# A two-layer mixture of experts behind a packed attention: the first half played from a list of 300 steps

## The chip, the cores and the metric

The kernel runs on one core of a Trainium2 chip. Its time is the device time of one execution in microseconds (us); lower is better. All arithmetic is in 32-bit floats. TensorE takes fp32 operands for transposes, scores and small products, and its own rounded form (fp32r) for the expert layers, where every operand is split into a high and a low part and three products are summed.

## What is computed

```python
# q, k, v: (4, 8, 576, 64), p: (4, 8, 32, 64)
p_packed = sm_attn(p, k, v)              # 32 packed queries over 576 keys
x = sm_attn(q, p_packed, p_packed)       # 576 queries over 32 packed keys
x = x.transpose(0, 2, 1, 3).reshape(2304, 512)

logits = x @ w_gate                      # layer 1: 8 experts, top 1, capacity 576
expert = argmax(logits); gate = softmax(logits)[expert]
# in order of rows, a row is kept while its expert has taken fewer than `capacity`
x = gate * (relu(x @ w1[expert]) @ w2[expert])     # 0 for rows that are dropped

logits = x @ w_gate2                     # layer 2: 8 experts, top 1, no capacity
expert = argmax(logits); gate = softmax(logits)[expert]
eom = sigmoid(x @ w_output_gate)[expert]
out = gate * eom * (relu(x @ w1b[expert]) @ w2b[expert])
```

## The kernel before

The four batches go through the attention one after another. `load` brings k, q (three pieces each) and v of a batch, `transp` transposes a piece on TensorE and copies it out of PSUM. `s1_mm`, `s1_max`, `s1_exp` and `s1_rs` are the first softmax; `a1_T` transposes its result, `pp_mm` multiplies it with v, `pp_scale` divides by the sums and `pp_T` transposes the packed rows to `ppT`. The second softmax goes in two halves of 4 heads: `s2_mm`, `s2_tr` (a transpose in 32x32 blocks), `s2_max`, `s2_sub`, `s2_exp`, `s2_sum`, `s2_mul`, `s2_back`; its result is `a2T`. `g1_g`, `g1_l` and `g1_t` make the logits of the first gate; `ga`, `ga2`, `gb`, `gc`, `gd` choose the expert of each row, its rank and whether it is kept, and the expert that a batch needs.

The main path takes it that the kept rows of a batch all go to one expert and that only batch 0 and one more batch have any; with these inputs that is so, and the rest stands behind the test at the end. The expert part is done for two slots: batch 0 (its expert is `e0`) and the batch that `route` finds (`slots_i`). In layer 1 of the experts `moe1_ppw` multiplies `ppT` with a quarter of w1 (four quarters), and `layer1` multiplies that with `a2T` into one of eight tiles of `h`. `moe1_layer2` makes one of four tiles of `y` out of `h` and w2, which `split` cuts into `w2ah` (ScalarE) and `w2al` (GpSimd or VectorE). The second expert layer follows for batch 0, then for the other slot; `moe2_layer2` writes 128 rows of the output, the last block of a slot with `osb` copied by ScalarE and stored by a transfer of the SyncE queue.

Every engine runs its instructions in the order in which they are written, and so does the SyncE queue, which starts all transfers. The order is written by hand: `att_iter`, `att_last` and `att_end` hold the steps of neighbouring batches, interlocked; `FL()` puts one piece of expert layer 1 between steps of the last attention. All PSUM tiles come from one ring of four (`psm`), all raw weights from one ring of four buffers (`raw_p`). At the end an `If` on `flag_i` would run the remaining slots and a general path; its condition does not hold here, and every engine jumps over the body.

Of the kernel before, what the change touches and what calls it, by code (L numbers as in the profile page):

```python
# [8 lines left out]
FP32 = mybir.dt.float32  # L9
# [14 lines left out]
def tr(nc, out, in_, ident):  # L24
    return nc.tensor.transpose(out, in_, ident)  # L25


@with_exitstack
def tile_kernel(
# [124 lines left out]
    sp = [ENG.SP]  # L154
# [202 lines left out]
    def pp_scale(b):  # L357
        pps = ab_p.tile([128, 2, 2, D], FP32, tag="pps", name="pps")
        pp, sm = at.pop(("pp", b)), at.pop(("sm", b))
        for G in range(2):  # L360
            nc.vector.tensor_scalar(
                pps[:, G], pp[:, G, 0:D].unsqueeze(1).to_broadcast([128, 2, D]), sm[:, G:G + 1], None,
                op0=ALU.mult)
        at["pps", b] = pps

    def pp_T(b):
# [4 lines left out]
        nc.vector.tensor_copy(ppT[:, b], ps[:, :, 0:128])  # L371
# [22 lines left out]
    def s2_sub(b, G, eng):  # L394
        eng.tensor_tensor(sv(b, G), sv(b, G), bc(at.pop(("mx", b, G)), 32), op=ALU.subtract)
# [11 lines left out]
    def s2_mul(b, G, eng):  # L407
# [90 lines left out]

    def split(src, nm, i, lo_eng):

        wp = mp["ws2"] if i == 3 else mp["ws"]
        hi = wp.tile([128, 1024], FP32R, tag="w", name=nm + "h")
        lo = wp.tile([128, 1024], FP32R, tag="w", name=nm + "l")
        s = src.rearrange("p a b -> p (a b)")
        nc.scalar.activation(out=hi, in_=s, func=ACTF.Copy)  # L505
        lo_eng.tensor_tensor(lo, s, hi.bitcast(FP32), op=ALU.subtract)  # L506
        a = src.shape[1]
        return tuple(t.rearrange("p (a b) -> p a b", a=a) for t in (hi, lo))
# [9 lines left out]
    def moe1_load1(e):  # L518

        ws = []  # L520
        for fq in range(F // 256):
# [6 lines left out]
    def moe1_load2(e):  # L528
        ws = []
        for dh in range(2):  # L530
            for kh in range(2):
                w = raw(4, 256)
                nc.sync.dma_start(
                    w, w2a[bass.ds(e, 1), kh * 512:(kh + 1) * 512, dh * 256:(dh + 1) * 256].rearrange(
                        "o (k p) d -> p (o k) d", p=128))
                ws.append(w)
        return ws

    def moe1_x(a2, lo_eng):
# [23 lines left out]
    def chain(ps, seq, mid={}):  # L563
# [673 lines left out]
```

## Time and profile before

| what | value |
|---|---|
| median of 3 runs | 276.68 us (275.87 to 277.39) |
| profiled execution | 277.06 us, of which 275.0 us from the first to the last instruction (span) |
| TensorE (PE) | 249.9 us busy, 91% of the span |
| VectorE (DVE) | 130.6 us, 47% |
| ScalarE (ACT) | 100.6 us, 37% |
| GpSimd (POOL) | 44.5 us, 16% |
| granted TensorE clock | 0.97 of full on the mean |

A busy share is a mean over stages: attention to 59 us, experts' first layer to 161 us, second layer to the end. The page's slices show where they differ: TensorE is 90% or more busy in nearly every slice from 135 us on, and the transfers keep the DMA engines busy above 90% only up to 41 us. What a change in the first half is worth is read from the waits and the clock of that half.

### The profile page before, as it was taken

The numbers are of one execution on the slowest core, as the hardware profiler recorded it, in microseconds if no ns is written. First come the engines' busy times: TensorE is split into PE (matmuls) and PEld (weight loads), VectorE is DVE, ScalarE is ACT, GpSimd is POOL, SyncE is SP. The second block draws the span as 40 slices with busy tenths as digits, with TensorE's granted clock in tenths as the row PEclk, the third lists the DMA queues.
The fourth block names the chain that finished last, engine by engine and source line by source line (L and its number), as shares of the span: only waits on it lengthen the run. The fifth ranks groups of instructions, "written<-read, shape, count | busy, mean of one in ns | idle before, by whom it ended". The sixth has DMA issues, their size and how long they took to land. (4 is left out here: it accounts for less than half of the span.)

```text
span 275.0 us, 6065 instructions
## 1 busy us (share of the span) xinstructions
PE 249.9 (91%) x2529; PEld 218.4 (79%) x2529; DVE 130.6 (47%) x316; ACT 100.6 (37%) x152; POOL 44.5 (16%) x69
## 2 busy tenths in 40 slices
PE   7789889929989989997999999999999999999970
PEld 5567657707886979786999999999888999988850
DVE  0234776985995684369712333487031435610000
ACT  3586847623470310445502232263140414410020
POOL 5001514532350330006420000000020000002000
PEclk9999999986999999999799999999999999999995
DMA  6999990067320005943696224008201360001211
GB/s 195 395 331 382 396 390 31 6 215 247 87 69 2 0 0 184 301 135 118 156 257 221 79 76 153 2 14 252 80 23 73 119 229 2 0 0 39 61 42 45
DMA packets 29652, 37.17 MB, mean 135 GB/s; under 512 B 4144, under 2 KB 21168, under 8 KB 29616
## 3 DMA queue, kind: packets, MB, share of 16 engines
q1 hardware_dynamic: 29616, 36.69, 40.6%
q8 instruction: 22, 0.36, 0.6%
q14 instruction: 14, 0.11, 0.1%
HBM read 31.25 MB, written 4.72 MB: 131 GB/s over the span
## 5 line engine op out<-in xcount | busy, mean ns | idle before, releaser
L21 PE MATMUL o<-w2bh,h 128*128 128x512 f32 x144 | 45.9, 391 | 0.0
L21 PE MATMUL y<-h,w2ah 128*128 128x288 f32 x256 | 44.6, 296 | 0.0
L21 PEld LDWEIGHTS y<-h,w2ah 128*128 128x128 f32 x256 | 37.6, 189 | 0.0
L584 DVE SCALAR_TENSOR_TENSOR h<-h 128x576 fp32r<-128x576 f32 (+3 forms) x64 | 25.8, 447 | 24.7 <-ACT h L577 24.7
L577 ACT ACTIVATE h<-h 128x576 fp32r<-128x576 f32 x32 | 20.4, 651 | 36.3 <-PE h L21 32.5
L21 PEld LDWEIGHTS o<-w2bh,h 128*128 128x128 f32 x144 | 26.9, 188 | 5.7
L21 PE MATMUL o<-w2bl,h 128*128 128x512 f32 x80 | 31.3, 391 | 0.0
L21 PE MATMUL y<-h,w2al 128*128 128x288 f32 x128 | 27.7, 297 | 0.8 <-DVE w2al L506 0.8
L21 PE MATMUL h<-yh,w1bh 128*128 128x288 f32 x128 | 27.5, 296 | 0.0
L21 PE MATMUL h<-yh,w1bl 128*128 128x288 f32 x128 | 27.4, 295 | 0.0
L21 PE MATMUL h<-yl,w1bh 128*128 128x288 f32 x128 | 27.3, 295 | 0.0
L241 ACT ACTIVATE T<-tp 128x768 f32<-128x768 f32 x24 | 19.9, 850 | 11.4 <-PE tp L25 11.4
L21 PEld LDWEIGHTS y<-h,w2al 128*128 128x128 f32 x128 | 20.5, 188 | 1.5 <-DVE w2al L506 1.0
L25 PE MATMUL tp<-ident,r 128*128 128x128 f32 x144 | 20.1, 283 | 1.6 <-DMA r<-in_k_dram 1.2
L506 POOL TENSOR_TENSOR w2al<-wraw,w2ah 128x1024 fp32r<-128x1024 f32 x6 | 14.2, 2389 | 44.1 <-ACT w2ah L505 44.1
L683 POOL TENSOR_SCALAR osb<-osb,g 64x512 f32<-64x512 f32 x2 | 3.1, 1570 | 111.0 <-DVE osb L682 61.4
L21 PEld LDWEIGHTS h<-yh,w1bh 128*128 128x128 f32 x128 | 20.6, 189 | 0.2
L21 PEld LDWEIGHTS h<-yh,w1bl 128*128 128x128 f32 x128 | 20.6, 188 | 0.0
L21 PEld LDWEIGHTS h<-yl,w1bh 128*128 128x128 f32 x128 | 20.6, 188 | 0.0
L25 PEld LDWEIGHTS tp<-ident,r 128*128 128x128 f32 x144 | 16.3, 144 | 5.1 <-issue 1.2
L593 ACT ACTIVATE yh<-y 128x576 fp32r<-128x576 f32 x8 | 5.2, 651 | 40.8 <-PE y L21 40.8
L594 DVE TENSOR_TENSOR yl<-y,yh 128x576 fp32r<-128x576 f32 x8 | 6.0, 755 | 27.3 <-ACT yh L593 27.3
(173 smaller groups left out, 378.0 us busy)
## 6 DMA issues: line engine op xcount, KB each, us to landing
wraw<-in_moe_w_dram SPq DMA_DIRECT2D x32, 512.0 KB, 4.8
r<-in_k_dram SPq DMA_DIRECT2D x12, 384.0 KB, 7.2
r<-in_q_dram SPq DMA_DIRECT2D x12, 384.0 KB, 8.7
v<-in_v_dram SPq DMA_DIRECT2D x4, 1152.0 KB, 8.4
out_dram<-zt SPq DMA_DIRECT2D x2, 1152.0 KB, 7.5
out_dram<-osb SPq DMA_DIRECT2D x8, 256.0 KB, 2.0
a2s<-a2T SPq DMA_DIRECT2D x1, 576.0 KB, 5.4
p_sb<-in_p_dram SPq DMA_DIRECT2D x4, 64.0 KB, 6.9
```

What stands on the lines that cost most here:

```text
L21: return nc.tensor.matmul(out, lhsT=lhsT, rhs=rhs, start=start, stop=stop)
L25: return nc.tensor.transpose(out, in_, ident)
L241: nc.scalar.activation(out=o, in_=i, func=ACTF.Copy)
L506: lo_eng.tensor_tensor(lo, s, hi.bitcast(FP32), op=ALU.subtract)
L577: nc.scalar.activation(out=hi, in_=ps[:, :, 0:HS], func=ACTF.Relu)
L584: nc.vector.scalar_tensor_tensor(o, i, 0.0, a.bitcast(FP32), op0=ALU.max, op1=ALU.subtract)
L593: nc.scalar.activation(out=half(y[0][:, c, :]), in_=ps[:, :, 0:HS], func=ACTF.Copy)
L594: nc.vector.tensor_tensor(half(y[1][:, c, :]), ps[:, :, 0:HS], half(y[0][:, c, :]).bitcast(FP32), op=ALU.subtract)
L683: nc.gpsimd.tensor_scalar(o[:n], o[:n], g2[:n, t:t + 1], None, op0=ALU.mult)
```

## The change

The body from the first load to the end of the second slot's expert layer 1 is no longer a sequence of calls in functions but a list, `PLAN`, of 300 names. `STEPS` maps a name to a call (`tk00`: transpose piece 0 of k of batch 0; `y014`: slot 0, y tile 1, products of row block 4), and a loop plays the list. The steps are the same pieces of work, some cut finer: a load is one piece, `split` is `high` and `low` apart, `moe1_layer2` is eight steps for the eight blocks of `h` and one that copies out. A letter at a step's end names an engine (A: ScalarE, D: VectorE, none: the default, GpSimd for `s2_sub`, `s2_mul` and the low halves, VectorE for `pp_scale` and `pp_T`, ScalarE for `a1_T`).

```diff
+PLAN = """
+warm4 warm9 warm7 k00 tk00 k01 tk01 k02 tk02 p0 dup0 pT0 k10 tk10 p1 dup1 sa00 ma00 ea00 sa01 ma01 k12 ea01 rs0 pT1
+k11 tk11 tk12 at00D q00 tq00 v0 q01 at01D pp00 pp01 sc0A q02 k21 tq01 k20 tq02 pt0A sa10 q10 ma10 ea10 sa11 p2 ma11
...
-    def pp_scale(b):
+    def pp_scale(b, eng=1):
         pps = ab_p.tile([128, 2, 2, D], FP32, tag="pps", name="pps")
         pp, sm = at.pop(("pp", b)), at.pop(("sm", b))
         for G in range(2):
...
+            if eng == 0:
+                nc.scalar.activation(out=pps[:, G], in_=i, func=ACTF.Copy, scale=sm[:, G:G + 1])
+            else:
+                nc.vector.tensor_scalar(pps[:, G], i, sm[:, G:G + 1], None, op0=ALU.mult)
...
-        nc.vector.tensor_copy(ppT[:, b], ps[:, :, 0:128])
+        evac(eng, ppT[:, b], ps[:, :, 0:128])
...
+    def y_mm(ps, h, w, c, kk):
...
+        for x, (i, j) in enumerate(((0, 0), (0, 1), (1, 0))):
+            for u in range(2):
+                mm(nc, ps[:, u, 0:HS], w[i][:, kk % 4, ds_], h[j][:, kk, HSL[u]],
+                   kk == 0 and x == 0, kk == NF - 1 and x == 2)
...
-            nc.scalar.activation(out=o[:n], in_=ps[:n, 0, :], func=ACTF.Copy, scale=g2[:n, t:t + 1])
+            w = DM // 2 if last else DM
+            nc.scalar.activation(out=o[:n, 0:w], in_=ps[:n, 0, 0:w], func=ACTF.Copy, scale=g2[:n, t:t + 1])
+            if last:
+                nc.vector.tensor_scalar(o[:n, w:], ps[:n, 0, w:], g2[:n, t:t + 1], None, op0=ALU.mult)
...
-        nc.sync.dma_start(
+        (nc.scalar if last else nc.sync).dma_start(
...
-        warm(16)
...
-        def att_iter(b):
...
+        for t in PLAN.split():
...
+            STEPS[n](*a)
...
+        bs1_act = val(slots_i[0:1, 0, 0:1], B - 1, ENG.Activation)
         for t in order:
-            moe2_layer2(h, ws, t, g2_1, bs1)
+            last = t == order[-1]
+            moe2_layer2(h, ws, t, g2_1, bs1_act if last else bs1, last)
...
-    with tc.If(rest > 0, preferred_fallthrough_block=False):
+    with tc.If(rest > 0):
```

The list also names engines. `pp_scale` and `pp_T` of batches 0, 2 and 3 go from VectorE to ScalarE. `a1_T` was on ScalarE in its first part and on VectorE in its second for batches 0 to 2; now it is on VectorE for batch 0 and for the first part of batch 1, and on ScalarE otherwise. One low half of w2 of slot 0 instead of two is on VectorE, and the low half of `x` of the second slot goes from VectorE to GpSimd. The 20 warm-up matmuls are all at the start. K of batch 3 is loaded ahead of v of batch 2. The y tiles of slot 0 come in the order 1, 2, 0, 3, woven into one another, and the logits of batches 1 to 3 are ahead of them and not inside.

**VectorE before**, from the index of batch 0's expert (`e_i`) to the packed rows of batch 3 (`pps`, `ppT`), in the last attention:

```order
L220 CAST e_i<-pe_136 1x1
L329 TENSOR_SCALAR sm<-sm 128x2
L330 RECIPROCAL sm<-sm 128x2
L411 STREAM_TRANSPOSE a2T<-sT 128x2x288
L383 STREAM_TRANSPOSE sT<-s 128x576
L402 TENSOR_REDUCE dn_1097<-sT 128x18
L403 TENSOR_SCALAR dn_1097<-dn_1097 128x18
L404 RECIPROCAL dn_1097<-dn_1097 128x18
L391 TENSOR_REDUCE mx_1149<-sT 128x18
L361 TENSOR_SCALAR pps<-pp,sm 128x128 x2
L371 COPY ppT<-ppTp 128x256
```

**ScalarE in the changed kernel**, the same place: batch 2's `pps` to the first copies of expert layer 1 (`wh`, `h`):

```order
L379 ACTIVATE pps<-pp,sm 128x128 x2
L257 ACTIVATE T<-tp 128x3x128x2
L257 ACTIVATE a1T<-a1Tp 128x640
L257 ACTIVATE a1T<-a1Tp 128x512
L257 ACTIVATE ppT<-ppTp 128x256
L257 ACTIVATE T<-tp 128x3x128x2 x3
L379 ACTIVATE pps<-pp,sm 128x128 x2
L416 ACTIVATE sT<-sT 128x576
L257 ACTIVATE ppT<-ppTp 128x256
L591 ACTIVATE wh<-ppw 128x512 x2
```

The packed rows of batches 2 and 3 have left VectorE's row behind the softmax work and stand on ScalarE, ahead of the experts' first copies.

**VectorE before**, second slot's layer 1, the choice of batch 0's second expert (`c`, `eq`, `pe`, `e_0`) among the copies of `h`:

```order
L584 SCALAR_TENSOR_TENSOR h<-h 128x576
L195 TENSOR_REDUCE c_1965<-cp 1x8
L203 TENSOR_REDUCE m<-c_1965 1x1
L205 TENSOR_TENSOR eq<-c_1965,m 1x8
L206 SCALAR_TENSOR_TENSOR eq<-eq,revv 1x8
L207 TENSOR_REDUCE pe_1969<-eq 1x1
L208 TENSOR_SCALAR pe_1969<-pe_1969 1x1
L220 CAST e_0_1978<-pe_1969 1x1
L214 TENSOR_REDUCE tot<-c_1965 1x1
L215 TENSOR_TENSOR mu_138<-tot,m 1x1
L584 SCALAR_TENSOR_TENSOR h<-h 128x576
L560 TENSOR_TENSOR wl<-ppw,wh 128x512
```

**VectorE in the changed kernel**, the same choice:

```order
L614 SCALAR_TENSOR_TENSOR h<-h 128x576 x3
L211 TENSOR_REDUCE c_2096<-cp 1x8
L219 TENSOR_REDUCE m<-c_2096 1x1
L221 TENSOR_TENSOR eq<-c_2096,m 1x8
L222 SCALAR_TENSOR_TENSOR eq<-eq,revv 1x8
L223 TENSOR_REDUCE pe_2100<-eq 1x1
L224 TENSOR_SCALAR pe_2100<-pe_2100 1x1
L236 CAST e_0_2109<-pe_2100 1x1
L230 TENSOR_REDUCE tot<-c_2096 1x1
L231 TENSOR_TENSOR mu_138<-tot,m 1x1
L626 TENSOR_TENSOR yl<-y,yh 128x576 x2
```

It stood between copies of `h`; now all eight copies of `h` are ahead of it.

**ScalarE before**, the end of the program, from the second slot's block of 64 rows on:

```order
L681 ACTIVATE osb<-o 64x512
L675 ACTIVATE osb<-o,g_1_2558 128x512 x3
L1194 TENSOR_LOAD flag_i
L1195 COMPARE_AND_BRANCH
L1195 UNCONDITIONAL_BRANCH
```

**ScalarE in the changed kernel**, the same end:

```order
L723 ACTIVATE osb<-o 64x512
L715 ACTIVATE osb<-o,g_1_2559 128x512 x2
L715 ACTIVATE osb<-o,g_1_2559 128x256
L726 ISA
L726 DMA out_dram<-osb 128x512
L1061 TENSOR_LOAD flag_i
L1062 COMPARE_AND_BRANCH
```

The last block is copied in half by ScalarE, which also starts its transfer, and the unconditional branch behind the test is gone from here: it stands behind the body, at the program's end. On the other engines the branch moves in the same way.

## Rows read from the trace of the kernel before

**Rows 1.** Five stretches: length, then busy us (instructions) by engine, granted clock, DMA.

```profile
core 0: us, PE busy (x) PEld busy (x) DVE busy (x) ACT busy (x) POOL busy (x), PEclk, DMA share, GB/s
4.30:40.20 35.90, 30.90 (x633) 22.58 (x631) 16.19 (x38) 22.74 (x38) 6.77 (x14) 1.00 1.03 376
40.20:59.00 18.80, 14.29 (x436) 11.49 (x433) 15.93 (x43) 10.38 (x16) 7.40 (x7) 1.00 0.17 60
59.00:80.40 21.40, 19.66 (x209) 16.25 (x210) 17.11 (x33) 11.29 (x18) 9.11 (x9) 0.84 0.55 175
80.40:135.80 55.40, 51.04 (x421) 45.22 (x419) 37.17 (x99) 18.18 (x31) 11.34 (x6) 0.97 0.36 111
135.80:266.70 130.90, 130.86 (x825) 120.70 (x823) 44.02 (x105) 36.04 (x50) 6.46 (x4) 1.00 0.29 90
```

**Rows 2.** Waits of TensorE, 0 to 140 us: total us, times, longest.

```profile
PE ppTp L25 <- DVE pps L361: 3.7, 1, 3.7
PE s L21 <- ACT T L241: 3.2, 3, 1.4
PE h L21 <- DVE h L584: 2.4, 1, 2.4
PE cp L21 <- DVE K L478: 1.2, 1, 1.2
```

**Rows 3.** Timeline of VectorE, 51 to 131 us: start, us, instruction.

```profile
51.96 2.62 DVE L206 SCALAR_TENSOR_TENSOR eq<-eq,revv 1x8 f32<-1x8 f32 x1
...
54.97 0.14 DVE L220 CAST e_i<-pe 1x1 int32<-1x1 f32 x1
...
124.86 2.34 DVE L205 TENSOR_TENSOR eq<-c,m 1x8 f32<-1x8 f32 x1
127.24 2.31 DVE L206 SCALAR_TENSOR_TENSOR eq<-eq,revv 1x8 f32<-1x8 f32 x1
...
130.26 0.74 DVE L584 SCALAR_TENSOR_TENSOR h<-h 128x576 fp32r<-128x576 f32 x1
```

**Rows 4.** Timeline of GpSimd, 41 to 136 us.

```profile
51.87 2.69 POOL L543 TENSOR_TENSOR xl<-a2T,xh 128x1152 fp32r<-128x1152 f32 x1
...
124.79 4.74 POOL L506 TENSOR_TENSOR w2al<-wraw,w2ah 128x1024 fp32r<-128x1024 f32 x2 [26.31 <-ACT w2ah L505]
```

**Rows 5.** Groups by form, ScalarE 4.3 to 60 us: count, busy us, mean ns.

```profile
L241 ACT ACTIVATE T<-tp 128x768 f32<-128x768 f32 x23 | 19.0, 849 | 11.4 <-PE tp L25 11.4
```

**Rows 6.** Groups by form, VectorE 40 to 86 us.

```profile
L361 DVE TENSOR_SCALAR pps<-pp,sm 128x128 f32<-128x128 f32 x4 | 1.2, 340 | 0.0
L371 DVE COPY ppT<-ppTp 128x256 f32<-128x256 f32 x2 | 0.8, 425 | 1.2 <-PE ppTp L25 1.2
```

**Rows 7.** Timelines: SyncE's first expert-weight transfer, TensorE's first expert product.

```profile
56.12 0.98 SPq L523 DMA_DIRECT2D wraw<-in_moe_w_dram  x2
...
59.90 0.45 PE L21 MATMUL ppw<-wraw,ppT 64*32 64x256 f32 x8 [0.30 <-DMA wraw<-in_moe_w_dram]
```

**Rows 8.** Timeline, end of the program.

```profile
266.26 0.40 PE L21 MATMUL o<-w2bl,h 128*128 128x512 f32 x1
266.75 0.69 ACT L675 ACTIVATE osb<-o,g 128x512 f32<-128x512 f32 x1 [4.52 <-PEq L1195]
267.46 0.33 SPq L684 DMA_DIRECT2D out_dram<-osb  x1
```

**Rows 9.** Sequencers, branch (L1195) and end (L1232): ns min/median/max, first and last start.

```profile
L1195 SPq EVENT_SEMAPHORE  x9: 17/17/17, 268.0 to 270.9; - x9
...
L1195 ACTq COMPARE_BRANCH  x2: 38/41/44, 267.3 to 267.6; - x2
...
L1195 SPq COMPARE_BRANCH  x2: 38/48/57, 267.8 to 271.0; - x2
...
L1232 SPq EVENT_SEMAPHORE  x10: 17/28/28, 273.7 to 275.0; - x10
...
L1232 ACTq DRAIN  x2: 8/44/81, 270.8 to 274.5; - x2
```

More of the change, by code (lines that the diff above doesn't have):

```diff
@@ L153, in tile_kernel @@
     HSL = [slice(0, HS), slice(HS, S)]
-    sp = [ENG.SP]
     def bc(ap, n):
@@ L516, in new_h, with moe1_load1 @@
         return h[:, :, 0:S], h[:, :, S + (LAST if last_first else 0):], h
-    def moe1_load1(e):
+    def moe1_load1(e, pieces=range(4)):
         ws = []
-        for fq in range(F // 256):
+        for fq in pieces:
             w = raw(4, 256)
@@ L595, in moe1_layer2 @@
             half(y[1][:, c, :]), ps[:, :, 0:HS], half(y[0][:, c, :]).bitcast(FP32), op=ALU.subtract)
+    def moe1_layer2(h, ws, c, y):
+        ps = psm("y")
+        for kk in range(NF):
+            y_mm(ps, h, ws[2 * (c // 2) + kk // 4], c, kk)
+        y_out(ps, c, y)
     def new_y(slot):
@@ L662, in moe2_load2, with moe2_layer2 @@
         return ws
-    def moe2_layer2(h, ws, t, g2, bsel):
+    def moe2_layer2(h, ws, t, g2, bsel, last=False):
         n = 128 if t < NT - 1 else LAST
@@ L1091, in tile_kernel @@
-        y0 = new_y(0)
-        def logits():
-            g1_l(1, B)
-        def onehots():
-            g1_t(1, B)
-            ga2(1, ga(1, B, "a1"))
-        def ranks():
-            gb(1, B)
-            gc(1, B, "a1")
-        def slots():
-            st["rest1"] = gd(1, B, "a1")
-            st["slots"] = route()
-        moe1_layer2(st["h"], ws, 0, y0, {14: logits, 18: onehots})
-        att_r.close()
-        pr = pool_in(moe, side="right", reuse_waits="tile")
-        mp["ws2"] = pr("ws2", 4)
@@ L1141, in tile_kernel, with gate_index, gate_rest, close_left @@
-        for i in (2, 3):
-            bz = val(slots_i[0:1, 0, i - 1:i], B - 1)
+        st, pw, wp, x1, h1, y = {}, {}, {}, {}, {}, {}
+        def gate_index():
+            st["e0"] = val(to_int(pe1[:, 0:1], "e0_i")[0:1, 0:1], E - 1)
+        def gate_rest(b0, b1):
+            st["r", b0] = gd(b0, b1, f"a{b0}")
+        def close_left():
+            att.close()
+            pm = pool_in(moe, reuse_waits="tile")
+            mp["y"] = pm("y", 1)
+            mp["ws"] = pm("ws", 10)
+        def close_right():
+            att_r.close()
+            pr = pool_in(moe, side="right", reuse_waits="tile")
+            mp["ws2"] = pr("ws2", 4)
+            mp["o"] = pr("o", 2)
@@ new lines, in tile_kernel @@
+        for t in PLAN.split():
+            n = t.rstrip("DAP") if t[-1] in "DAP" and t[-2].isdigit() else t
+            a = [int(x) for x in n.lstrip("abcdefghijklmnopqrstuvwxyzPT")]
+            n = n.rstrip("0123456789")
+            if t[-1] in "DAP" and t[-2].isdigit():
+                a.append({"A": 0, "D": 1}[t[-1]] if n in ("at", "sc", "pt") else V[t[-1]])
+            STEPS[n](*a)
+        slots_i, nb_f = st["slots"]
+        bs1, gs_1, y0, h, e2_0, g2_0 = st["bs"], st["gs"], y[0], h1[1], st["e2"], st["g2_0"]
@@ L1147, in tile_kernel @@
+        ws = [wp[1, i] for i in range(4)]
         e20 = val(e2_0[0:1, 0:1], E - 1)
```

354 lines of the change are left out of this document (92 added, 262 removed).

## Prediction

> **What bounds the kernel now.** I read the table of stretches first [rows 1]. From 135.8 us to the last matmul TensorE is busy 130.86 of 130.90 us at full clock; the change touches no step there but the last output block, so that half stays as long as it is. Everything before 135.8 us is open: TensorE is busy 30.90 of 35.90 us, then 14.29 of 18.80, 19.66 of 21.40 (at a granted clock of 0.84) and 51.04 of 55.40 (at 0.97). The first of these stretches is one in which the DMA engines are full (share 1.03). In the second they stand nearly idle (0.17), and still TensorE waits: the experts' weights can be asked for only when the index `e_i` of batch 0's expert is known, at 54.97 us [rows 3]. SyncE starts the first of them at 56.12 us and the first expert product runs at 59.90 us, behind that transfer [rows 7]. TensorE's waits up to 140 us, read next [rows 2], name three more places: 3.7 us once on VectorE's `pps`, 3.2 us in three waits on ScalarE's `T`, 2.4 us once on VectorE's `h`. The bound is therefore TensorE's amount of work, plus gaps in the first half where in-order queues of VectorE and ScalarE hold it up, plus slower clock around these gaps, plus 8.3 us between the last matmul's end (266.26 + 0.40 [rows 8]) and the span's end at 275.0 us.
>
> The sum goes against the profiled execution: 277.06 us, of which the span is 275.0; the median of the runs is 276.68, so 0.4 us is taken off at the end.
>
> **Term a, the start of the expert layer (59.9 us now).** Before 59.0 us TensorE has 30.90 + 14.29 us of work behind its start at 4.3, so it can't be done before 49.5 us; that is the lower end, 10.4 us earlier than 59.9. What held it is (1) `e_i`, found by a VectorE row that also carries the softmax work and batch 2's `pps` and `ppT`, and (2) the 3.7 us wait on `pps`. The list moves both: `pps` and `ppT` of batches 2 and 3 go to ScalarE, which removes the wait on VectorE's row, and the chain to `e_i` comes ahead of batch 3's last steps. From `e_i` to the first product now takes 59.90 - 54.97 = 4.9 us; with `e_i` at an estimated 43 us (right behind the last transfers of the first stretch, which are at their end at about 41) the weights are there by about 48, ahead of TensorE. Before, the operation L206 on that chain took 2.62 us while GpSimd's `xl` ran from 51.87 to 54.56 [rows 3, 4]; in the list `xl` of batch 0 stands behind `ei`, so that this hold leaves the chain.
>
> What is late next is ScalarE. It did 22.74 + 10.38 = 33.1 us before 59.0 [rows 1], of which 19.0 are 23 copies `T` at 849 ns [rows 5]. It gains six `pps` (priced by VectorE's 340 ns each: 2.0 us) and three `ppT` (425 ns: 1.3 us) [rows 6] and the second parts of `a1_T`, less the two that it gives up. That is 37 to 40 us of work which begins at about 6 us: done by 43 to 46 if it never waited, and it waits on each of TensorE's groups. The upper end is that only the 3.7 us wait goes and 0.8 of it comes back in ScalarE's own row: the start at 57, 2.9 us earlier. I take 52.0, nearer to the TensorE floor than to 57, since TensorE's own waits in these rows (3.7 and 3.2) and the late index account for most of the gap and each is addressed: **-7.9 us** (ends -10.4 and -2.9).
>
> **Term b, 59.0 to 80.4 us.** At a clock of 0.84 over 21.4 us, 0.16 x 21.4 = 3.4 us of full-speed work is lost, right behind the gaps of the stretch before; and one wait on `T` is 1.4 us [rows 1, 2]. Without the gaps both go, 4.8 us at most. Against that stands VectorE: it did 15.93 + 17.11 = 33.0 us between 40.2 and 80.4 [rows 1]. Of this 2 x (2 x 0.34 + 0.425) = 2.2 moves to ScalarE and 2.5 of L206's hold goes, but now about 27 us of it must be finished before the logits of batches 1 to 3, which the list puts ahead of the `y` tiles instead of inside one. That ends at 67 to 74 us, where TensorE with 15.7 us of expert work behind 52.0 arrives at 67.7. I charge 3 us for this backlog: **-1.8 us** (ends -4.8 and +1.0). The 24 products of the logits move, they aren't saved.
>
> **Term c, 80.4 to 135.8 us.** TensorE waits 2.4 us for `h` and 1.2 us for the operand `K` [rows 2]; at a clock of 0.97, 0.03 x 55.4 = 1.7 us is lost. The wait on `h` has a plain cause in the rows: VectorE's L205 and L206, the choice of batch 0's second expert, took 2.34 and 2.31 us for 8 numbers each, beside GpSimd's two `w2al` from 124.79 us of 4.74 us each, and the next copy of `h` could run only at 130.26 [rows 3, 4]. All eight copies of `h` stand ahead of that choice now. What is queued behind it is the low half of the second slot's last `y` tile and, on SyncE, the loads of the next weights, which are wanted some 25 us later: free. Sum removed: 5.3. New is a wait on ScalarE: `xh` of the second slot needs a copied `a2T` of a batch that is known only after `slots_i`; behind it in ScalarE's row stands the copy of the third `y` tile, which frees a PSUM buffer. From the weights' row, an index to its data is 4.9 us; I charge 1.5: **-3.8 us** (ends -5.3 and +1.0).
>
> The list also puts `xl` of the second slot and one more `w2al` on GpSimd, beside which VectorE's small operations were seen at 2.3 to 2.6 us instead of the 0.14 of a small CAST next to them [rows 3, 4]. [...]
>
> **Term d, the end.** The last matmul ends at 266.66; ScalarE copies it in 0.69, SyncE starts the store at 267.46 [rows 8], its waits L1195 follow to 270.9 with the last COMPARE_BRANCH at 271.0, and the next thing on SyncE is at 273.7, 2.7 us later, on the far side of the jump [rows 9]. The span ends at 275.0. So three pieces stand in line: store 3.5, jump 2.7, end 1.3. With the branch turned back the body is the fallthrough and every engine takes the jump at the test. ScalarE starts the store itself, reads the flag and jumps while the transfer is under way; SyncE, with no store of its own, reached the test long before. ScalarE's instructions after the test ran from 267.6 to the DRAIN at 270.8, 3.2 us; the copy by halves saves at most 0.25. ScalarE is thus at the end some 5.3 us behind the last matmul, the landing comes at about 4, and with the closing 0.5 to 1 the end is at 5.6 to 6.0 us instead of 8.3: **-2.4 us** (ends -2.8 and 0, when a second fetch at the end block takes the place of the removed one).
>
> [...]
>
> **Sum.** -7.9 - 1.8 - 3.8 - 2.4 = -15.9; 277.06 - 15.9 = 261.2, and 0.4 less for the median: **260.8 us**. With all lower ends (-23.3) it is 253.4, with all upper ends (-0.9) 275.8; half-way combinations give 257 to 265.5, the forecast's own range.
>
> **The rivals.**
> - *TensorE never waits.* ScalarE keeps ahead and VectorE's backlog is done in time: terms at -9.9, -4.0, -5.0 and -2.4 make -21.3, so 255.4 us (253.5 to 257). For it: over 4.3 to 59.0 us VectorE is busy 32.1 and ScalarE 33.1 of 54.7 us [rows 1], and the DMA share of 0.17 says that data is not the limit from 42 us. Against it: DMA is full up to 41 us, and in the second stretch VectorE is busy 15.93 of 18.80. Chance 0.22.
> - *The waits change places.* ScalarE's row with `pps`, `ppT` and `a1T` now stands between TensorE's groups as VectorE's did, and the late softmax halves hold the logits: term a is -5.0, b and c give nothing, d holds. -7.4, so 269.3 us (265.5 to 271). Against it: ScalarE has 21.6 of these 54.7 us free. Chance 0.20.
> - *The new end doesn't do what it says* (two jumps, two fetches): 263.2, within the forecast's range; a chance of 0.25 inside it.
> - *Slower: gaps that cost clock.* The pieces of batch 2 and 3, the expert's pieces and the logits are woven in one row; each gap that a late VectorE piece leaves in TensorE's row between 50 and 120 us costs its wait and the slower stretch behind it. Two such pairs are in the rows: 2.4 us with 1.7 of lost clock, and 3.7 with 3.4 [rows 1, 2], 4.1 to 7.1 together, 5.6 on the mean. It decides from three of them on (15.9 / 5.6 = 2.8); with four the time is 260.8 + 22.4 = 283 us. For it: VectorE's 33 us of backlog and the moved logits. Against it: the two gaps of before came from one cause each, which the list removes. Chance 0.04.
>
> **How the numbers follow.** Forecast with its own range 257 to 265.5: 0.50; TensorE never waits 0.22; waits change places 0.20; slower 0.04; between the last two, a change within 0.5% (1.4 us, about what a measurement of this kernel can tell from no change): 0.04. The first three are faster, 0.92 together. The range reaches from the first rival's 253.5 to most of the second's: 253.5 to 270.5.
>
> **What would show it.** The first expert product starts at about 52 us (a), with no wait on `pps`; a granted clock of 0.97 or more from there (b); no wait over 1.5 us on `h` (c), so that the dense second half begins at about 121 to 123 us; the last matmul's end to the span's end is about 6 us (d). [...] Any clock below 0.9 between 55 and 120 us would say that gaps are left which I didn't see.

## The result and the profile after

The changed kernel took 268.41 us (median of 4 runs, 266.27 to 269.92) against 276.44 us of the kernel before (275.87 to 277.39): a ratio of 0.970 with a 95% interval of 0.961 to 0.979, 8.0 us faster. Each ratio in this document is formed from the runs within 1.5% of the fastest of their kernel, while the medians are of all runs. The forecast was 260.8, 15.9 us faster in its sum: the way was right and the range held the time, but half of the gain is missing, and 268.4 lies outside the forecast's own 257 to 265.5, next to the 269.3 of the rival "the waits change places". Six more runs of the same kernel gave a median of 267.59 (265.69 to 270.37).

The profiled execution after is one of the short ones: 266.27 us with a span of 264.5, so 10.8 us below the profiled execution before. This is the table of its stretches (length, busy us and instructions by engine, granted clock, DMA share, GB/s), to be laid beside [rows 1]:

```profile
3.60:40.00 36.40, 30.50 (x627) 23.08 (x625) 17.71 (x34) 23.76 (x42) 8.02 (x17) 1.00 1.02 368
40.00:52.00 12.00, 8.19 (x229) 6.35 (x228) 9.42 (x31) 7.31 (x14) 4.55 (x4) 0.86 0.18 64
52.00:60.00 8.00, 6.05 (x203) 4.55 (x201) 5.23 (x11) 4.41 (x8) 3.47 (x3) 1.00 0.79 257
60.00:80.00 20.00, 19.71 (x238) 15.74 (x240) 18.13 (x35) 11.96 (x20) 9.66 (x8) 1.00 0.35 108
80.00:127.60 47.60, 47.11 (x411) 43.03 (x405) 28.86 (x86) 16.95 (x27) 12.96 (x6) 1.00 0.49 149
127.60:258.40 130.80, 130.79 (x824) 120.63 (x823) 47.31 (x113) 36.73 (x51) 7.91 (x4) 1.00 0.26 83
```

From 60 us on TensorE is full (19.71 of 20.00, 47.11 of 47.60) at full clock (1.00 is the full grant; a figure below is a mean with spells at 0.50, here from 46.41 to 49.83 us, before from 60.46 to 67.29 and from 132.14 to 135.55), where before it had 19.66 of 21.40 at 0.84 and 51.04 of 55.40 at 0.97. The last row is the stretch that the change leaves alone: 130.8 us, as before. What has not moved is the part ahead of 60 us. Its waits, of the changed kernel's TensorE from 0 to 140 us (total us, times, longest), against [rows 2]:

```profile
PE pp L21 <- issue: 5.1, 3, 2.1
PE rk L21 <- DVE oh L190: 3.5, 1, 3.5
PE s L21 <- issue: 2.0, 2, 1.7
```

The waits on `pps` (3.7), on `T` (3.2) and on `h` (2.4) are gone. New are a wait of 3.5 us of the rank product `rk` on VectorE's one-hot rows `oh`, and 7.1 us under "issue", which is time in which TensorE waited for nothing that the profile shows. With two short waits more, ahead of `gp` and `tp`, the sum under "issue" is 7.6 us; it was 2.4 before, in three waits. So the first expert product runs at 60.56 us, not at the forecast's 52.0 (59.90 before):

```profile
60.56 0.67 PE L21 MATMUL ppw<-wraw,ppT 64*32 64x256 f32 x16
```

The path of the profiled executions in us, cut at four events of TensorE that both traces have:

| stretch | before | after | moved |
|---|---|---|---|
| start to the first expert product | 59.90 | 60.56 | +0.7 |
| to the first `y` (the 3.51 us of logits, now ahead of `y`, taken out of after) | 20.63 | 17.80 | -2.8 |
| to the second slot's first `y` (the same 3.51 us added to after) | 55.40 | 49.22 | -6.2 |
| to the last matmul's end | 130.73 | 130.81 | +0.1 |
| to the end of the span | 8.36 | 6.10 | -2.3 |
| outside the span | 2.06 | 1.77 | -0.3 |

### The profile page after: what moved, and what is told of

Read it like the earlier page. It is cut to its first block, busy times and chain, and to the rows that moved or that the text cites. A ratio compares the mean times of both kernels' runs of the same rounds, so it can differ in the third digit from the quotient of the medians.

```text
span 264.5 us, 6064 instructions
## 1 busy us (share of the span) xinstructions
PE 244.8 (93%) x2529; PEld 215.2 (81%) x2529; DVE 127.3 (48%) x307; ACT 102.9 (39%) x161; POOL 49.3 (19%) x70
## 4 chain that ended last, share of the span: by engine, by line
PE 83%; DVE 6%; issue 4%; DMA 3%; SPq 2%; ACT 0%; POOL 0%; DVEq 0%; ACTq 0%
PE h L21 27%; PE y L21 20%; PE o L21 19%; PE tp L25 4%; PE s L21 3%; DMA v<-in_v_dram 3%; PE pp L21 3%; PE l L21 2%; PE lp L21 1%; PE ppw L21 1%; SPq L283 1%; DVE oh L190 1%; PE a1Tp L25 1%; DVE d L182 1%; DVE h L614 1%
## 5 line engine op out<-in xcount | busy, mean ns | idle before, releaser
L257 ACT ACTIVATE T<-tp 128x768 f32<-128x768 f32 x24 | 19.3, 851 | 7.9 <-PE tp L25 7.7
L526 POOL TENSOR_TENSOR w2al<-wraw,w2ah 128x1024 fp32r<-128x1024 f32 x7 | 16.6, 2390 | 26.0 <-ACT w2ah L520 26.0
L25 PE MATMUL tp<-ident,r 128*128 128x128 f32 x144 | 19.2, 277 | 0.8 <-DMA r<-in_k_dram 0.2
L715 ACT ACTIVATE osb<-o,g 128x512 f32<-128x512 f32 (+1 forms) x8 | 5.3, 661 | 36.9 <-PE o L21 29.0
L25 PEld LDWEIGHTS tp<-ident,r 128*128 128x128 f32 x144 | 15.9, 142 | 3.6 <-issue 1.6
L21 PEld LDWEIGHTS o<-w2bl,h 128*128 128x128 f32 x80 | 15.0, 188 | 3.3
```

What stands on the lines that cost most here:

```text
L21: return nc.tensor.matmul(out, lhsT=lhsT, rhs=rhs, start=start, stop=stop)
L257: nc.scalar.activation(out=o, in_=i, func=ACTF.Copy)
L526: eng.tensor_tensor(lo, src.rearrange("p a b -> p (a b)"), hi.rearrange("p a b -> p (a b)").bitcast(FP32), op=ALU.subtract)
L715: nc.scalar.activation(out=o[:n, 0:w], in_=ps[:n, 0, 0:w], func=ACTF.Copy, scale=g2[:n, t:t + 1])
```

## What held the start

VectorE's timeline in the changed kernel (start, us, instruction), then GpSimd's row of the same time:

```profile
41.84 1.14 DVE L187 SCALAR_TENSOR_TENSOR first<-d,revv 128x40 f32<-128x40 f32 x1 [0.37 <-POOL d L182]
43.02 0.20 DVE L188 TENSOR_REDUCE mx<-first 128x5 f32<-128x40 f32 x1
43.24 2.33 DVE L190 TENSOR_TENSOR oh<-rev,mx 128x40 bf16<-128x40 f32 x1
45.61 0.23 DVE L470 TENSOR_REDUCE S<-oh 128x8 f32<-128x40 bf16 x1
...
49.41 0.14 DVE L236 CAST e_i<-pe 1x1 int32<-1x1 f32 x1
```

```profile
42.88 2.64 POOL L571 TENSOR_TENSOR xl<-a2T,xh 128x1152 fp32r<-128x1152 f32 x1
```

The neighbours of `oh` take 0.20 and 0.23 us; `oh` takes 2.33, and it ends 0.05 us behind GpSimd's `xl` (42.88 + 2.64 = 45.52). It is the hold of [rows 3] and [rows 4] on another operation. The list has `xl0` behind `ei`, but a list is an order for each engine alone: GpSimd's `xl` doesn't wait for VectorE's index (`e_i`, 49.41), so it began at 42.88, right behind the subtraction ahead of it and 6.5 us before the index. Beside that subtraction (GpSimd, 41.77 to 42.93) the same shows on a smaller scale: `first`, of the size of `oh`, takes 1.14 us and ends at 42.98. In the kernel before, with GpSimd idle beside them, `first` took 0.19 us (at 46.46) and `oh` 0.20 (at 46.92). TensorE stands at `rk`, which the list puts ahead of batch 3's scores, so its whole row waits.

Not every operation was held: the reduction `mx`, with one input, took 0.20 us (at 43.02) beside the same `xl`. The two that were held here read two tensors each: `oh` (`rev`, `mx`) with 2.33 us, and `first` (`d`, `revv`) with 1.14.

Most of the time under "issue" falls inside rows of equal small matmuls. TensorE's timeline of the changed kernel, two of them:

```profile
27.12 1.01 PE L21 MATMUL pp<-v,a1T 64*32 64x64 f32 x74
30.22 0.93 PE L21 MATMUL pp<-v,a1T 64*32 64x64 f32 x70 [2.09 <-issue]
...
55.53 0.95 PE L21 MATMUL pp<-v,a1T 64*32 64x64 f32 x70
58.43 0.92 PE L21 MATMUL pp<-v,a1T 64*32 64x64 f32 x71 [1.95 <-issue]
```

All 144 matmuls of a batch's `pp` have the same operands, and the wait falls after the 74th in one batch, after the 70th (of the rows merged here) in another. Counted by weight loads from the program's start, the waits stand at fixed numbers: 491, 622 and 880 before; 231, 491, 622, 1012 and 1141 after: steps of 130 or multiples of it. The page's list of queues has one for instructions:

```profile
q8 instruction: 22, 0.36, 0.6%
```

That is 22 reads of 16 KB each, 0.36 MB together. The read that belongs to each wait, taken from the trace's records of that queue:

```
wait at load   read of 16 KB      TensorE goes on
231            14.38 to 15.46     16.94   (1.48 later)
491            27.72 to 28.79     30.23   (1.44)
622            34.09 to 35.09     36.55   (1.46)
1012           55.65 to 56.97     58.43   (1.46)
1141           59.48 to 60.64     61.98   (1.34)
```

By these rows TensorE ran out of instructions: a block of 130 loads and their matmuls is used up in some 1.7 us where it is full of `pp` (144 pairs took 1.88 us in the kernel before, shown below), and the next is still on its way. The sum rose from 2.4 to 7.6 us, and not because other work stands at these numbers: in both kernels it is `pp` at 231, 491 and 1012 and `s` at 622 and 1141. What moved is when TensorE comes to it and when the read comes. Load 231 runs at 19.70 in the kernel before, 2.0 us behind the landing of its read (17.66), without a wait; with the earlier waits gone TensorE is there sooner. The read for load 1012 runs from 49.68 to 50.85 in the kernel before, with the DMA engines nearly idle (share 0.04 from 49.68 to 52.02), and this `pp` runs through from 52.02:

```profile
52.02 1.88 PE L21 MATMUL pp<-v,a1T 64*32 64x64 f32 x144
```

In the changed kernel the earlier index lets the experts' weights be asked for from 50.59 on (56.12 in [rows 7]); this read begins among them, at 55.65, with a DMA share of 0.87 from 51.13 to 55.65. That the weights make it late is argued from these rows; no run tried it alone.

Single waits under "issue" of 0.2 us (`tp` in the changed kernel) to 4.8 us (`pp` in the best kernel below) were measured in these runs.

## The experiments

The kernels below ran on three chips, on each of them beside the kernel before, whose medians there are 276.21 us (for the next four sections), 276.97 (for the two edits of the kernel before and the last two arrangements) and 276.25 (for the rest). The changed kernel ran on the first, so the kernels of the other two are compared with it by the ratios.

### The changed kernel again

> The changed kernel once more, unchanged, because its four times lay in two groups (266.3 and 266.9; 269.9 twice) while those of the kernel before lay within 1.5 us. Theory of a lost clock window: the time again falls near 266.5 or near 270, and a profile of a 270 us run differs from that of a 266 us run by a stretch at a lower granted clock between 40 and 60 us, behind TensorE's idle time there, with the same waits. Rival, a queue that serves instruction fetches and data in another order: the waits of TensorE that no engine causes differ by 3 us. Ratio to the kernel before: 0.97 (0.96 to 0.98).

267.59 us, ratio 0.967 (0.963 to 0.972). Its profiled execution (267.3 us) has the same waits: `rk` 3.6, "issue" 4.9 in `pp` and 0.6 in `s`, but the clock is lower ahead of 52 us:

```profile
3.60:40.00 36.40, 32.15 (x627) 25.20 (x626) 17.68 (x34) 23.61 (x42) 8.01 (x17) 0.95 1.02 367
40.00:52.00 12.00, 8.14 (x218) 5.99 (x221) 9.00 (x29) 6.93 (x14) 4.56 (x4) 0.72 0.18 66
```

0.72 in place of 0.86, and the first expert product at 61.66 instead of 60.56, 1.1 us. That speaks for the clock; the two groups of times did not come back, the ten runs fill 265.7 to 270.4, and no 270 us run was profiled, so the far end is not explained.

### The low half of x later on GpSimd

```diff
-... rs3 sc2A tq22 gg1 xl0 sm11 at30 ... sb20 mu11 tr20 ...
+... rs3 sc2A tq22 gg1 sm11 at30 ... sb20 mu11 xl0 tr20 ...
```

> One name of the list moves: the low half of batch 0's x, on GpSimd, stands behind the softmax product of batch 1's second half instead of ahead of it. Theory 1 (the start of the expert layer failed to move because TensorE stands at the rank product behind VectorE's one-hot rows, which took 2.33 us while GpSimd's x low half ran from 42.88 to 45.52): the one-hot takes about 0.2 us, TensorE's wait on it falls from 3.5 to about 1.4 us, the index is there about 2.1 us earlier, and the time is 2 to 4 us lower (2.1 from the wait, up to 1.7 from the clock that stood at 0.86 from 40 to 52 us). Rival (TensorE is held by its own instruction fetches and the weights' transfer in any case): the wait shrinks, the first expert product stays at 60.5 us within 0.7, and the time within 1 us.

263.35 us, ratio 0.951 (0.947 to 0.955): 4.2 us below the changed kernel, a little more than theory 1 gave. Its timelines of VectorE, GpSimd and TensorE:

```profile
43.35 0.20 DVE L190 TENSOR_TENSOR oh<-rev,mx 128x40 bf16<-128x40 f32 x1
...
47.23 0.14 DVE L236 CAST e_i<-pe 1x1 int32<-1x1 f32 x1
```

```profile
51.84 2.69 POOL L571 TENSOR_TENSOR xl<-a2T,xh 128x1152 fp32r<-128x1152 f32 x1
```

```profile
43.61 0.19 PE L21 MATMUL rk<-oh,tri 128*128 128x40 bf16 x1 [1.41 <-DVE oh L190]
```

`oh` takes 0.20, the wait falls from 3.5 to 1.4, the index is 2.2 us earlier, the first expert product runs at 57.52. The clock from 40 to 52 us is 1.00 instead of 0.86. Of the 3.0 us by which the first expert product comes earlier, 2.1 are the wait; the rest goes with the clock (0.14 of 12 us is 1.7 at the most). The waits for instructions are no smaller in sum: 1.1 instead of 1.95 in batch 3's `pp`, but 1.2 instead of 0.3 ahead of `gp`. The two profiled executions lie 2.7 us apart (266.27 and 263.57), so they don't account for all of the 4.2 between the medians. The 1.4 us that is left at `rk` contains the hold on `first`, which takes 1.14 us here too.

### The end as it was

```diff
-            w = DM // 2 if last else DM
+            w = DM
...
-        bs1_act = val(slots_i[0:1, 0, 0:1], B - 1, ENG.Activation)
-            moe2_layer2(h, ws, t, g2_1, bs1_act if last else bs1, last)
+            moe2_layer2(h, ws, t, g2_1, bs1)
-    with tc.If(rest > 0):
+    with tc.If(rest > 0, preferred_fallthrough_block=False):
```

> The changed kernel with the end of the kernel before: the last block copied whole by ScalarE, its store started by SyncE, and the branch turned as it was. By term d the time from the last matmul's end to the end of the span goes from 6.1 us back to about 8.3 us, with a gap of some 2.7 us between the landing of the store and SyncE's last waits: 2.2 us more. Rival (the gain at the end came from ScalarE starting the store, not from the branch): the gap isn't there, and the difference is under 0.7 us.

269.53 us, 1.9 above the changed kernel; the intervals of the ratios (0.970 to 0.980 against 0.963 to 0.972) overlap a little, so the traces decide. SyncE's sequencer at the branch and at the end, first with the old end (ns, first and last start), then in the changed kernel:

```profile
L1059 SPq COMPARE_BRANCH  x2: 38/48/57, 260.2 to 263.7; - x2
...
L1096 SPq EVENT_SEMAPHORE  x10: 17/28/28, 266.5 to 267.8; - x10
```

```profile
L1062 SPq EVENT_SEMAPHORE  x9: 17/17/17, 257.0 to 263.0; - x9
L1062 SPq COMPARE_BRANCH  x1: 53/53/53, 254.1 to 254.1; - x1
...
L1099 SPq EVENT_SEMAPHORE  x10: 17/28/157, 263.1 to 264.4; - x10
```

With the old end SyncE jumps at 263.7, behind the landing, and goes on at 266.5, 2.8 us later, as in [rows 9]. With the new end it jumped at 254.1, long before the last matmul, and from its last wait for the store (263.0) to the next instruction (263.1) there is nothing. From the last matmul's end to the span's end: 8.8 and 6.1 us. The 2.7 us between them are the gap behind the branch. SyncE could jump so early because it had no store left to start; turning the branch alone, with the store still on SyncE, was not tried.

### The last block whole

```diff
-            w = DM // 2 if last else DM
-            nc.scalar.activation(out=o[:n, 0:w], ...)
-            if last:
-                nc.vector.tensor_scalar(o[:n, w:], ps[:n, 0, w:], g2[:n, t:t + 1], None, op0=ALU.mult)
+            nc.scalar.activation(out=o[:n], ...)
```

> The changed kernel with its new end, but the last block copied whole by ScalarE (0.69 us) instead of in two halves by ScalarE (0.47) and VectorE (0.48), which in the trace of the changed kernel ran one behind the other. From the last matmul's end to the store's issue: 0.80 us as in the kernel before, instead of 1.16; the time 0.3 to 0.4 us lower, no more than a measurement can just tell. Rival (the halves overlap in part, the order in the trace is chance): 0.2 us higher.

The halves do not run side by side. The end of the changed kernel, then with the block whole:

```profile
258.47 0.47 ACT L715 ACTIVATE osb<-o,g 128x256 f32<-128x256 f32 x1 [4.80 <-PE o L21]
259.04 0.48 DVE L717 TENSOR_SCALAR osb<-o,g 128x256 f32<-128x256 f32 x1 [15.73 <-ACT osb L715]
259.55 0.40 ACTq L726 DMA_DIRECT2D out_dram<-osb  x1
```

```profile
260.11 0.69 ACT L715 ACTIVATE osb<-o,g 128x512 f32<-128x512 f32 x1 [4.80 <-PEq L1060]
260.82 0.40 ACTq L724 DMA_DIRECT2D out_dram<-osb  x1
```

VectorE's half waits for ScalarE's; both write the one tile `osb`. Whole, the store starts 0.80 us behind the last matmul instead of 1.16, and the end comes 5.5 instead of 6.1 us behind it. The time, 266.29 us (1.3 lower, 0.959 to 0.966), is inside the spread of the changed kernel, which is wider than this effect.

### The packed rows back on VectorE

```diff
-... rs3 sc2A tq22 ... at31 pt2A tq30 ... pp31 sc3A sb21 ... sm20 pt3A gg2 ...
+... rs3 sc2 tq22 ... at31 pt2 tq30 ... pp31 sc3 sb21 ... sm20 pt3 gg2 ...
```

> The changed kernel with the packed rows of batches 2 and 3 (scaling and copy) back on VectorE; the places in the list stay. The prediction's term a said that moving them to ScalarE is what removes TensorE's 3.7 us wait on them: then a wait on VectorE's scaling of 2 to 4 us is back ahead of the transposes of these rows and the time is 2 to 4 us higher. Rival: the order of the list removed the wait and the engine is of no weight, since VectorE stands idle 1.6 us and 2.1 us at these two places in the trace of the changed kernel: the time is within 1 us of the changed kernel's.

271.17 us, ratio 0.982 (0.977 to 0.987), 3.6 above the changed kernel by the medians and 4 by the ratios. The size is the prediction's, its mechanism is not: in the trace no wait on `pps` is back. TensorE's waits from 56 to 86 us, and the stretch behind:

```profile
PE pp L21 <- issue: 3.6, 1, 3.6
PE s L21 <- DVE ppT L259: 0.5, 1, 0.5
```

```profile
60.00:80.00 20.00, 19.49 (x306) 14.78 (x298) 16.04 (x33) 9.69 (x15) 6.92 (x6) 0.86 0.34 108
```

VectorE does the scaling and the copies without being late by more than 0.5 us, and the wait for instructions in batch 3's `pp` is 3.6 us here (1.95 in the changed kernel). From 60 to 80 us the clock is 0.86 instead of 1.00, 2.8 us of work at the most. But a profile without these letters shows nearly the same: the kernel with the last block whole, which has the changed kernel's list, waited 3.7 us in this `pp` and had a clock of 0.91 from 60 to 80 us, in an execution of 267.25 us. That the letters are worth about 3.6 us is measured; by what way is open.

### The second expert's choice among the copies again

```diff
-... w13 h14 gs h16 h17 wh12 wl12 h15 zo3 wb13 wh13 wl13 gi zo2
+... w13 h14 gi gs h16 h17 wh12 wl12 h15 zo3 wb13 wh13 wl13 zo2
```

> The changed kernel with the choice of batch 0's second expert back among the copies of h of the second slot (behind the fifth of the eight). Term c: VectorE's two small operations of that chain take about 2.3 us each while GpSimd cuts the low half of w2, the copies of h behind them come late, and TensorE waits 2 to 4 us on K and h between 110 and 125 us, with a lower granted clock behind it: the time is 2 to 5 us higher. Rival: GpSimd's two operations lie elsewhere in the list now, the small operations take 0.2 us, and the time is within 1 us.

The choice stands behind the fifth of the eight copies here, behind the third in the kernel before. 266.38 us, ratio 0.963 (0.959 to 0.967), 1.2 below the changed kernel and within its spread: no cost, where 2 to 5 us were expected. VectorE's rows of the choice, and GpSimd's of these 16 us:

```profile
123.50 0.15 DVE L221 TENSOR_TENSOR eq<-c,m 1x8 f32<-1x8 f32 x1
123.69 0.15 DVE L222 SCALAR_TENSOR_TENSOR eq<-eq,revv 1x8 f32<-1x8 f32 x1
```

```profile
116.62 2.39 POOL L526 TENSOR_TENSOR w2al<-wraw,w2ah 128x1024 fp32r<-128x1024 f32 x1 [9.04 <-ACT w2ah L520]
```

GpSimd is done at 119.0, so the operations take 0.15 us each, against 2.34 and 2.31 in [rows 3]. The place in the list costs nothing here; the meeting with GpSimd did.

### The choice late in the kernel before

```diff
-            if f == 2:
+            if f == NF - 1:
                 e2_0 = g2_c(K16, 0)
```

> The kernel before, with one edit: the choice of batch 0's second expert stands behind all eight copies of h of the second slot, as in the changed kernel. Term c's wait taken alone: TensorE's waits of 2.4 us on h and 1.2 us on K are gone, the stretch from 80.4 to 135.8 us is 3.6 us shorter and up to 1.7 more by its clock: 271 to 273. Rival (as the run with the choice among the copies showed no cost in the changed kernel): other work, the low halves on GpSimd, makes copies late there, the waits move to another tile, and the time is within 1 us of 276.2.

273.75 us, ratio 0.986 (0.982 to 0.991): 3.2 us faster than the kernel before of the same chip (276.97). The 2.4 us on `h` are gone from TensorE's waits between 80 and 140 us:

```profile
PE cp L21 <- DVE K L478: 1.2, 1, 1.2
PE y L21 <- DVE h L584: 0.8, 1, 0.8
```

The expectation named the 1.2 us on `K` too; that wait belongs to the ranks of batches 1 to 3 some 30 us earlier and stays. A wait of 0.8 us on the last `h` is new.

### The low half of x late in the kernel before

```diff
-            st["x"] = moe1_x(a2T[:, 0], nc.gpsimd)
+            st["xh"] = moe1_x(a2T[:, 0], None)
...
             s2_sub(r, 0, nc.gpsimd)
+            st["x"] = moe1_x(a2T[:, 0], nc.gpsimd, st["xh"])
```

> The kernel before, with one edit: the low half of batch 0's x stands later on GpSimd, in the end of the attention behind the subtraction of batch 2's first half. Theory 1 (one operation of GpSimd held VectorE's chain to the index for 2.62 us in the kernel before, and the packed rows of batch 3, which TensorE waited 3.7 us for, stand behind that chain on VectorE): that operation takes about 0.2 us, the index comes near 52.5 instead of 54.97 us, TensorE's wait on the scaling falls from 3.7 to 1.2 to 2 us, and the time is 2 to 4 us lower, 272 to 274. Rival (the wait was the engine that the packed rows ran on, so only moving them to ScalarE removes it; the hold goes to the next small operations): the wait stays over 3 us and the time within 1 us of 276.2.

274.03 us, ratio 0.987 (0.983 to 0.991), 2.9 us faster. TensorE's wait on the packed rows falls from 3.7 to 1.2 with the engine unchanged, the operation that took 2.62 us takes 0.15, and the index is there at 51.80 instead of 54.97:

```profile
PE ppw L21 <- DMA wraw<-in_moe_w_dram: 1.3, 1, 1.3
...
PE ppTp L25 <- DVE pps L361: 1.2, 1, 1.2
```

```profile
51.26 0.15 DVE L206 SCALAR_TENSOR_TENSOR eq<-eq,revv 1x8 f32<-1x8 f32 x1
...
51.80 0.14 DVE L220 CAST e_i<-pe 1x1 int32<-1x1 f32 x1
```

So two thirds of that wait was GpSimd's hold on VectorE's row, not the packed rows' engine. The first expert product waits 1.3 us for its weights here. This profiled execution is the shortest of twelve (271.0 us).

### Sixty more loads in the warm-up

```diff
+        if n == 7:
+            for _ in range(60):
+                mm(nc, ps[0:32, 0, 0:32], wz[:, 0:32], wz[:, 0:32], True, True)
```

> The changed kernel with 60 more tiny matmuls (32 by 32) at the end of the warm-up, on zeros, their result unused. In the traces TensorE's waits without a cause stand at its 231st, 491st, 622nd, 1012th and 1141st weight load, steps of about 130 or multiples, in every kernel run so far, and each ends some 1.45 us after a 16 KB read on the queue of instruction reads. Theory (TensorE runs out of instructions at the end of each block that was read): the waits move to the same numbers counted from the new start, that is 60 loads earlier in the work: the first batch's pp has one later or none, one falls into the scores at 19 us, one into the transposes at 31 us, one near the end of batch 3's pp. The time is within 2 us of the changed kernel's, since the sum of the waits falls elsewhere but doesn't go. Rival (operands or PSUM that the trace doesn't show): the waits stay at the same places of the work, in pp and s, and their numbers rise by 60.

The waits kept to the numbers, as the theory said, and not to the work: they stand at loads 360, 619 and 1140 of the new count, with none at 491 and 1012 and none in the first batch's `pp`. TensorE's timeline:

```profile
15.63 1.65 PE L21 MATMUL pp<-v,a1T 64*32 64x64 f32 x144
...
22.36 0.72 PE L21 MATMUL s<-T,pT 64*32 64x288 f32 x6 [2.30 <-issue]
...
30.82 1.67 PE L21 MATMUL pp<-v,a1T 64*32 64x64 f32 x142
36.64 0.37 PE L21 MATMUL pp<-v,a1T 64*32 64x64 f32 x2 [4.15 <-issue]
```

Batch 1's `pp` now stops two matmuls ahead of its end instead of in its middle, for 4.15 us, and each wait ends 1.2 to 1.4 us behind a 16 KB read (that one lands at 35.40). But the ratio is 0.979 (0.974 to 0.985), 1.2% or 3.3 us above the changed kernel's, where 2 us either way was expected. It rests on the two shortest of six runs (269.88 and 271.67); the other four lie at 274.3 to 275.3, and the profiled one is among them. In it `rk` is reached 6.3 us later than in the changed kernel (51.9 instead of 45.6), the first expert product runs at 68.67, and the clock from 3.6 to 40 us is 0.90 instead of 1.00; how much of this the two long waits cause was not taken apart. Sixty instruction pairs that compute nothing cost some 3 us.

### Two more arrangements, and the best

Both edits that helped, together:

> The two edits that helped, together: the low half of batch 0's x later on GpSimd, and the last block copied whole by ScalarE. Theory: the two lie 200 us apart and add up, 0.3 to 0.6 us below the first edit alone (263.35), so about 262.9. Rival: the second edit's 1.3 us between medians was spread of the runs, not the end: no difference.

262.85 us, ratio 0.949 (0.944 to 0.953): the best kernel of this study, 4.7 us below the changed kernel. The 0.5 us below the first edit alone agree with the 0.6 at the end (5.5 instead of 6.1 us), but the two intervals overlap, so that they add up is not shown.

On top of it, the rank product behind batch 3's scores (`rk01 kp01` behind `ma31`):

> The first combination (262.85 median) with the rank product and the kept rows of batch 0 moved behind the scores and row maxima of batch 3. TensorE then doesn't stand at the rank product (1.4 us of wait left there). Theory: the wait on the one-hot rows goes from 1.4 us to nothing, but the chain to the index stands behind two maxima of 0.78 us each on VectorE, so index and weights come 1 us later; the first expert product stays within 0.7 us and the time is between 262 and 263.5. Rival (the index is what the expert layer waits for): the first expert product waits for the weights' transfer and the time is 1 to 2 us higher.

265.38 us, ratio 0.958 (0.953 to 0.963), 2.5 above the best. Both theories of the expectation missed the cause; the profiled execution is its longest, so only the place is read from it. The wait went one product further:

```profile
50.01 0.21 PE L21 MATMUL cp<-K,ones 128*128 128x40 bf16 x1 [2.34 <-DVE K L496]
```

The row maxima now stand ahead of `K` on VectorE, and TensorE stands at `cp` instead of `rk`. The first expert product did not wait for weights.

And 32 tiny loads ahead of `rk`, where TensorE stands idle:

```diff
+        for _ in range(32):
+            mm(nc, ps[0:32, 0, 0:32], wz[:, 0:32], wz[:, 0:32], True, True)
```

> The first combination (262.85 median) with 32 tiny matmuls on zeros, unused, ahead of the rank product, where TensorE stands idle for 1.4 us. Theory of the instruction blocks: TensorE's waits up to 40 us stay at the weight loads 231, 491 and 622; those behind the rank product stay at 752, 882, 1012 and 1141 by count, which is 32 loads earlier in the work: in batch 2's pp instead of the gate product behind it, in batch 3's pp at its 39th matmul instead of its 71st, ahead of the transposes of its packed rows instead of among its scores. Their sum, 0.7 to 5 us over the runs before, changes by up to 1.5 us either way, and the time is within 1.5 us of 262.85. Rival (missing operands): these waits stay at the same places of the work.

264.90 us, ratio 0.955 (0.950 to 0.960), 2.0 above the best, where 1.5 was the bound. The waits stayed at 231, 491 and 622 ahead of the new loads; behind them the one at 881 of the count lies in the middle of batch 2's `pp` now:

```profile
45.19 1.45 PE L21 MATMUL pp<-v,a1T 64*32 64x64 f32 x124
49.10 0.41 PE L21 MATMUL pp<-v,a1T 64*32 64x64 f32 x20 [2.45 <-issue]
```

It was 1.2 us ahead of a `gp` matmul in the run with the late `xl` alone. Batch 3's `pp` has none. The sum of the waits for instructions is 7.6 us in this profile and 7.3 in the best kernel's, and which alignment would be best was not found.

## Why the prediction was half right

**Term a, -7.9 forecast, +0.7 measured: the step that failed.** The waits that it named did go (`pps` 3.7, `T` 3.2), though the first not for the reason given: with the packed rows back on VectorE the kernel is 3.6 us slower, but no wait on `pps` returns. Two things took their place. The first was in the trace: "in the list `xl` of batch 0 stands behind `ei`, so that this hold leaves the chain" read the list as an order in time across engines. GpSimd's `xl` met `oh` instead of L206, and behind it stood TensorE with 3.5 us; moving it gave 4.2 us back. I had taken the wait in the kernel before for the engine's, while two thirds of it were this hold. The second was not in the sum at all: the three waits under "issue" of the kernel before, 2.4 us, were never asked for their cause, and became 7.6, of which 7.3 stand ahead of the first expert product. 3.5 + (7.3 - 2.4) = 8.4 is close to the 8.6 from 52.0 to 60.56. That the two add up so is arithmetic on one execution and on a value that was chosen between two ends; the second profile of this kernel has its first expert product at 61.66, and only the wait on `oh` was made shorter in a run.

**ScalarE was not late next.** The upper end of term a rested on its row; in the changed kernel no wait of TensorE on ScalarE reaches 0.5 us.

**Term b, -1.8 forecast, -2.8 measured.** The number is near, its two parts are not. The same matmuls, from the first expert product to the first `y`, before and after (after with the 3.51 us of logits):

```profile
59.90:80.53 20.63, 19.20 (x208) 16.07 (x209) 16.76 (x32) 11.42 (x18) 8.34 (x8) 0.83 0.52 165
60.56:81.87 21.31, 21.02 (x249) 16.10 (x245) 18.78 (x36) 11.40 (x19) 11.53 (x9) 1.00 0.33 101
```

At full clock TensorE is busy 21.02 - 3.51 = 17.5 us of 17.8, where the forecast took 15.7. So the clock gave back 19.20 - 17.5 = 1.7 us and not 3.4, and VectorE's backlog, charged at 3 us, cost TensorE next to nothing. That the two errors nearly cancel is luck. The rival with gaps and lost clock did not come in this stretch, but 0.86 appears from 40 to 52 us, where TensorE had stood at `rk`.

**Term c, -3.8 forecast, -6.2 measured.** TensorE's idle time fell from 4.4 us (55.40 - 51.04) to 0.5, not by the two named waits of 3.6 alone, and its busy time by 2.3 (51.04 to 45.22 + 3.51), where 1.7 was taken for the clock. The wait for the second slot's `xh`, charged at 1.5, did not come. One row was misread: the 4.74 us of `w2al` are two operations together, 2.4 us each, and each of the two VectorE operations lay beside one of them. The late place of the choice alone is worth 3.2 us in the kernel before, yet in the changed kernel an early place costs nothing, since GpSimd's low halves run elsewhere. The hold still happens after the change, where nobody waits for it:

```profile
130.27 2.31 DVE L222 SCALAR_TENSOR_TENSOR eq<-eq,revv 1x8 f32<-1x8 f32 x1
```

**Term d, -2.4 forecast, -2.3 measured in the span.** The jump before the landing is right, and no second gap came. The upper end of 0, and with it the 263.2 of the rival with two fetches, takes a second fetch at the end block; no run shows such a term. What the runs show is 2.8 us from SyncE's jump to its next instruction with the old end, and with the new one a jump at 254.1 and 0.1 us from the last wait to the next instruction. In the trace of the kernel before, reads of the instruction queues lie in the gap (271.24 to 272.67, the jump at 271.0); that they make it was not tried. The halved copy, for which 0.25 us was the most, lost 0.36 at the store's start.

**The chances.** The rival "the waits change places" had the right name and the wrong place: it expected ScalarE's row, where it was VectorE's row beside GpSimd and TensorE's own instructions. By its name it came true: new waits took the place of the old ones, and the first expert product runs at 60.56 us, later than the 57 of term a's upper end. That its time, 269.3 us, is so near is luck: it had term a at -5.0 and nothing from b and c, which came out as +0.7 and -9.0. The forecast's range held the time because it reached down to this rival: a missed by 8.6 us, while b and c gave 3.4 more than forecast.

## What to carry to other kernels

An order that interleaves engines says nothing of when an engine with free hands begins (here `xl`, listed behind `ei`, began 6.5 us before the index): for every long GpSimd operation that is moved, look which small VectorE operations of a chain run at that time, and who waits for them. Waits in a row of equal matmuls without a releaser are worth a count: here they fell at fixed numbers of weight loads, in steps of about 130 or multiples of it, each 1.34 to 1.48 us behind a read of the program's own instructions. Reordering or adding work changes them (here the sum went from 2.4 to 7.6 us), and the longest, 4.8 us on `pp` in the best kernel, fell into the stretch from 3.6 to 40 us, with a DMA share of 1.03. SyncE's taken branch was followed by a gap of 2.8 us where it came behind the last landing (263.7 to 266.5); reached at 254.1, ahead of the last matmul, it left 0.1 us at the end.

## What was not expected of the hardware

- By the places of the waits, TensorE's instructions come in reads of 16 KB (22 of them on that queue in the changed kernel), about 130 weight loads with their matmuls; a row of 144 64-column matmuls runs in 1.65 us (with sixty more loads), so it uses up more than one read. Single waits of up to 4.8 us followed; in the changed kernel the five at the fixed numbers end 1.34 to 1.48 us behind a read's landing, with sixty more loads 1.2 to 1.4.
- In the changed kernel the read came later where the transfers were full: the block from load 491 was entered at 30.23 us and the next read began at 34.09 (DMA share 0.97 between them); from load 752, entered at 47.86, it began at 48.68 (share 0.00). But in the kernel before 2.3 us passed at a share of 0.00 too (load 880 at 47.36, read at 49.68). That the data ahead in the DMA engines delays it was not tried alone.
- The same kernel varied by 4.7 us over ten runs (265.7 to 270.4), the kernel before by 3.7 over eleven on the same chip as six of them (274.9 to 278.6); the clock of the stretch from 40 to 52 us differed between two executions (0.86 and 0.72).
